# Half-by-half phases for the Fourier table, and a new hand-searched order, in a long-convolution and token-MLP kernel

## Chip, cores and metric

The kernel runs on one core of a Trainium2 chip. The metric is the device time of one execution in microseconds; 3 runs of the kernel before gave a median of 176.52 us (176.28 to 176.68).

## What is computed

Two blocks over a sequence of S = 2048 tokens with D = 448 channels in bfloat16, each behind a layer norm and with a residual. Cut to what matters:

```python
def A(q, k, v, shift_k, ssm_k, ssm_D):
    k_shift = sum over t < 4 of k_pad[:, t:t+S] * shift_k[:, 3-t]     # short causal convolution
    kv = k_shift * v
    y = irfft(rfft(pad(kv)) * rfft(pad(ssm_k)))[:S]                   # long causal convolution, length S, per channel
    return q * (y + kv * ssm_D)
def B(x, w1, b1, w2, b2):
    h = layernorm(x)                                                  # over D
    u = gelu(einsum("bsd,sf->bdf", h, w1) + b1)                       # mixes the tokens, F = 1792
    return transpose(einsum("bdf,fs->bds", u, w2) + b2)
h   = x + A(layernorm(x), ...)
out = h + B(layernorm(h), ...)
```

## The kernel before

The sequence index is split in two digits, 128 partitions times R = 16. The long convolution is a two-stage Fourier transform made of matmuls. Its stages have tags in the code:

- **tables** (emit_tables): the twiddle table E (128 x 32 x 128, fp16) is made on the chip. For each half h of it, VectorE multiplies a row of frequencies with a row of positions into integer phases (L827, 128 x 1024), adds a quarter turn for the second copy (L831, 128 x 1024) and masks both (L834, 128 x 2048); ScalarE then takes the sine (L837). Half 0 holds the positions 0 to 7, half 1 those from 8 to 15. Smaller tables (FW, MA, MB, MN) are made beside it on GpSimd, VectorE and ScalarE, and an identity matrix for transposes.
- **loads** (emit_loads): SP's queue brings in the kernel rows ssm_k (four loads, L877), k (four, L888), v (four, L891), the shift weights (three small ones, L880 and L883), the row D (L895) and the bias vectors (L898, L900).
- **kT**: TensorE transposes the kernel rows (L1028) with a few filler matmuls between (L1015), and copies (L731 on VectorE, L728 on ScalarE) bring them out of PSUM.
- **kv**: k is transposed (L956), convolved with the shift weights by matmuls with diagonal blocks (L982), and multiplied with v (L997, VectorE only).
- **k1, u1**: first Fourier stage of the kernel and of kv (L1049), with evacuations (L1059; L1057 adds the row D and is on VectorE only, for the group i = 0 of the kernel), and re-ordering DMAs from GpSimd and SP (L1065).
- **k2, u2**: second stage (L1084), scaled on evacuation (L729, L732) or copied (L728, L731).
- **i1**: products of the spectra on VectorE (L1150), first inverse stage on TensorE (L1167), evacuations, re-ordering DMAs (L1189; the last pair L1179). Beside it, bits of other work: statistics of the input's layer norm (**q**, L1225), transposes of E (**ct**, L1098), normalised rows (**xn**).
- **i2**: last inverse stage (L1285, L1293), gate and residual (L1302, L1304, L1312, L1322), second layer norm (L1340 to L1371).
- **mlp**: first layer with L1418 and L1428, GELU (L1408), second layer L1440 and the last addition L1443.

Nothing of the order is written out directly. Each operation is recorded with what it reads and writes, and a list scheduler (class _Sched, method schedule) simulates five engines with fixed estimates of each operation's time, and decides the order in which each engine's instructions are issued. Its priorities are the table WHEN: each step of a tag has one number, and of the operations that are ready the one with the lowest number goes first. The table WHERE says for each operation that ScalarE or VectorE could do which of them does it: "a" is ScalarE, "d" VectorE, "f" leaves it to the scheduler, which gives it to VectorE only when ScalarE has a backlog. Engines execute in the order so fixed, and wait on semaphores for what they need. An operation can have two kinds of predecessors: "after" stands for finished data, and "safter" only says that the other instruction must have been issued and run its estimated time in the plan; it adds no semaphore wait.

In the kernel before, the keys of the two halves of the phases are 79 and 73, and VectorE does them in turns: multiply of one half, multiply of the other, and so on.

Of the kernel before, what the change touches and what calls it, by code (L numbers as in the profile page):

```python
# [9 lines left out]

ENGS = ("pe", "act", "dve", "pool", "sp")
WHEN = {
    "dummy": (47,),
    "tables": (135, 108, 181, 171, 72, 79, 73, 180,),
    "loads": (107, 115, 122, 123, 200, 184, 83, 229, 88, 228, 168, 189, 218, 146, 156,),
    "kv": (207, 113, 131, 199, 132, 198, 48, 195, 226, 81, 103, 104, 75, 128, 136, 158, 185,),
    "kT": (61, 49, 202, 64, 222, 190, 152, 76,),
    "k1": (110, 116, 150, 183, 105, 134, 140, 163, 62, 87, 98, 133, 89, 194, 170, 169,),
    "k2": (82, 85, 70, 84, 129, 145, 91, 161, 193, 192, 175, 179, 100, 121, 182, 230,),
    "u1": (71, 80, 97, 126, 130, 155, 148, 173, 174, 176, 196, 219, 69, 90, 142, 209,),  # L20
    "xload": (263, 214, 5, 112,),
    "bias": (178, 216,),
    "q": (213, 241, 186, 251, 240, 231, 252, 272, 287,),
    "u2": (102, 114, 221, 268, 191, 177, 31, 45, 125, 144, 66, 162, 94, 101, 298, 224,),
    "ew": (120,),
    "i1": (77, 34, 43, 86, 53, 215, 59, 143, 65, 165, 19, 141, 18, 37, 67, 206, 54,),
    "ct0": (201, 38,),
    "ct": (223, 137, 20,),
    "xn": (68, 187, 307, 21, 36, 277,),
    "w1a": (299, 6, 303, 24,),  # L30
    "warm": (301, 294,),
    "i2": (74, 56, 281, 32, 188, 172, 40, 291, 106, 304, 264, 4, 3, 23, 7, 99, 160, 151, 204, 42, 225, 93, 293, 309,
        284, 197, 35, 159, 259, 14, 205, 118, 245, 220, 44, 302, 58, 288, 2, 12, 253, 271, 269, 262, 242, 166, 22,
        265, 16, 157, 292, 0, 39, 60, 232, 17, 236, 119, 283, 55, 267, 15, 92, 13, 111, 285, 249, 296, 308, 41, 300,
        26, 276, 95, 25, 282, 52, 279, 63, 30, 57, 310, 149, 117, 11, 273, 295, 305, 210, 46, 257, 203, 29, 127, 290,
        255, 124, 109, 306, 167, 212, 10, 8, 9, 211, 28,),
    "w1b": (280,),
    "w2": (208,),
    "mlp": (96, 27, 78, 51, 138, 1, 50, 147, 286, 153, 139, 164, 297, 33, 227, 289, 217, 154, 418, 419, 420, 421,
        422, 423, 424, 425, 426, 427, 428, 429, 430, 431, 432, 433, 434, 435, 436, 437, 438, 439,),  # L40
}
WHERE = {
    "kv": "ddaadfdd",
    "kT": "ddfdfddd",
    "k1": "faffaffadfaa",
    "k2": "addfffdaffdafffd",
    "u1": "fafdffafafddfffa",
    "bias": "f",
    "u2": "aafafaaaffffffaf",
    "i1": "aaffffffaffaafaa",  # L50
    "ct0": "f",
    "ct": "aaf",
    "xn": "dafa",
    "i2": "adfadafaafaf",
}


# [515 lines left out]
def _build(nc, A_q, A_k, A_v, A_shift_k, A_ssm_k, A_ssm_D, B_w1, B_b1, B_w2, B_b2, out):  # L573
# [54 lines left out]
    with ctx:  # L628
        sch = _Sched(nc, ctx, n_dma_sems=112, small_off=SMALL)
        op = sch.op  # L630
# [106 lines left out]
        def emit_tables():  # L737
            N8 = 8192.0
            SC = (2.0 * math.pi / N8) * (1.0 - 2e-6)
            HALF = 8 * 128  # L740
            NB = 3 * 128
            o_fr = small(512)
            o_s = small(64)
# [6 lines left out]
            bias = view(o_b, [4], f32)  # L750
# [17 lines left out]
            for x in range(2):  # L768
# [3 lines left out]
                   w=[(o_fr, 512, "fr")], n=128, est=160.0)  # L772
# [3 lines left out]
               w=[(o_JK, 4)], est=1500.0)  # L776
# [3 lines left out]
               n=128, est=190.0)  # L780
# [3 lines left out]
               n=128, est=190.0)  # L784
# [32 lines left out]
            for i in (10, 11):  # L817
# [2 lines left out]
                   r=[(o_p + 16, 4), (o_p + 4 * i, 4)], w=[(o_p + 16, 4)], n=1)  # L820
            op("dve", lambda e, W: e.tensor_copy(out=pcf[:, 0:6], in_=pc[:, 4:10]), r=[(o_p + 16, 24)],
               w=[(o_p + 48, 24)], n=6)
            for h in range(2):
                sch.t0 = T_TH if h else -40.0
                o_ph = (o_pi, o_TK)[h]
                ph = view(o_ph, [2, 8, 128], i32)
                op("dve", lambda e, W, h=h, ph=ph: e.tensor_tensor(  # L827
                    out=ph[:, 1], in0=frow.unsqueeze(1).broadcast_to([128, 8, 128]),
                    in1=srow[:, 8 * h:8 * h + 8].unsqueeze(2).broadcast_to([128, 8, 128]), op=ALU.mult),
                   r=[(o_fr, 512), (o_s, 64)], w=[(o_ph + 4096, 4096)], n=HALF, kind="1x")  # L830
                op("dve", lambda e, W, ph=ph: e.tensor_scalar(  # L831
                    out=ph[:, 0], in0=ph[:, 1], scalar1=2048, scalar2=None, op0=ALU.add),
                   r=[(o_ph + 4096, 4096)], w=[(o_ph, 4096)], n=HALF)
                op("dve", lambda e, W, ph=ph: e.tensor_scalar(  # L834
                    out=ph, in0=ph, scalar1=8191, scalar2=None, op0=ALU.bitwise_and),
                   r=[(o_ph, 8192)], w=[(o_ph, 8192)], n=2 * HALF)
                op("act", lambda e, W, h=h, ph=ph: e.activation(  # L837
                    out=E[:, 16 * h:16 * h + 16, :].rearrange("p a (b c f) -> p a b c f", b=4, c=2).rearrange("p a b c f -> p (a b) c f"),
                    in_=ph.rearrange("p c r (g f) -> p c (r g) f", f=16).rearrange("p c g f -> p g c f"),
                    func=ACT.Sin, bias=bias[:, 0:1], scale=-SC),  # L840
                   r=[(o_ph, 8192), (o_b, 4)], w=[(o_E + 4096 * h, 4096)], n=2 * HALF)
# [661 lines left out]
```

## Time and profile before

| what | us |
|---|---|
| median of 3 runs | 176.52 |
| the profiled execution | 176.59 |
| its span in the trace | 174.70 |
| last kernel rows' transposes begin on TensorE | 11.72 |
| first stage-one matmul of the kernel | 13.69 |
| last re-ordering transfer issued | 76.28 |
| last inverse stage goes on after it | 80.36 |
| second MLP layer begins | 129.39 |
| last instruction of the chain ends | about 172.3 |

Times are from one profiled execution, counted from the span's start. "Busy" of an engine leaves out waits and issue of DMAs. The chain of waits is followed back from the last instruction. TensorE's matmuls are pipelined and their ends are modelled. The granted TensorE clock was 1.00 throughout.

Some rows of the groups of instructions that matter below (mean duration of one, in ns): L827 1224, L831 690, L834 1222, L837 2020, L731 644, L1057 1089, L1059 913 on ScalarE and 1085 on VectorE, L1150 1082. Waiting times: GpSimd's re-ordering DMAs waited 12.5 us for ScalarE's evacuations of stage one and 10.2 us for those of the inverse stage; TensorE waited 3.3 us for the last re-ordering transfers.

### The profile page before, as it was taken

How to read it: one execution, taken by the hardware profiler on the slowest of the kernel's cores; microseconds unless marked ns; L12 is line 12 of the kernel's file. 1: busy time of each engine (PE TensorE's matmuls, PEld its weight loads, DVE VectorE, ACT ScalarE, POOL GpSimd, SP SyncE). 2: the span in 40 equal slices, each digit the busy share in tenths (PEclk: the TensorE clock that was granted, in tenths of full speed). 3: DMA queues.
4: the chain of work that ended last, by engine and by line, in shares of the span. 5: the costliest groups of instructions: out<-in, count | busy, mean ns of one | idle time of the engine just before them, and what ended most of it. 6: DMA issues, size and time to landing. Idle time of an engine off the chain costs nothing.

```text
span 174.7 us, 3576 instructions
## 1 busy us (share of the span) xinstructions
PE 161.2 (92%) x1419; PEld 92.7 (53%) x1419; DVE 103.6 (59%) x192; ACT 89.4 (51%) x128; POOL 62.4 (36%) x160
## 2 busy tenths in 40 slices
PE   6999999899989997756999999999999999999993
PEld 2776835352323332422344545555567777777783
DVE  7998899878979898988998561000003132132231
ACT  3786767888999999873792664521220000000000
POOL 8355708672902548774589660000000000000000
PEclk9999999999999999999999999999999999999999
DMA  5999846791948764559999999930000111101111
GB/s 174 408 310 370 285 154 263 278 356 60 271 142 312 243 208 119 163 127 367 381 391 403 421 420 422 420 152 0 0 0 4 53 53 53 53 0 56 53 53 53
DMA packets 15516, 35.15 MB, mean 201 GB/s; under 512 B 3804, under 2 KB 9580, under 8 KB 15500
## 3 DMA queue, kind: packets, MB, share of 16 engines
q1 hardware_dynamic: 12348, 28.15, 44.2%
q0 software_dynamic: 3008, 6.69, 11.9%
q8 instruction: 11, 0.18, 0.4%
q10 hardware_dynamic: 144, 0.08, 0.2%
q14 instruction: 5, 0.04, 0.1%
HBM read 22.05 MB, written 1.84 MB: 137 GB/s over the span
## 4 chain that ended last, share of the span: by engine, by line
PE 60%; ACT 9%; DMA 9%; DVE 7%; POOL 6%; issue 5%; SPq 1%; POOLq 0%; DVEq 0%
PE ps L1440 24%; PE ps L1428 12%; PE ps L1418 8%; ACT arena L728 5%; DMA arena<-arena 5%; DMA arena<-in_A_ssm_k_dram 4%; PE ps L1049 4%; PE ps L1084 3%; ACT arena L1059 3%; DVE arena L1312 3%; POOL arena L1189 3%; PE ps L1285 2%; DVE arena L1371 2%; PE ps L1167 2%; PE ps L982 2%
## 5 line engine op out<-in xcount | busy, mean ns | idle before, releaser
L1443 DVE SCALAR_TENSOR_TENSOR arena<-ps,arena 128x448 bf16<-128x448 f32 (+2 forms) x17 | 11.1, 656 | 55.6 <-PE ps L1440 55.6
L1440 PE MATMUL ps<-arena 128*128 128x448 bf16 (+2 forms) x238 | 42.7, 342 | 0.0
L1440 PEld LDWEIGHTS ps<-arena 128*128 128x128 bf16 x238 | 33.3, 145 | 9.5
L728 ACT CAST arena<-ps 128x896 bf16<-128x896 f32 (+1 forms) x31 | 25.0, 954 | 1.0 <-PE ps L925 0.5
L1418 PE MATMUL ps<-arena 128*128 128x448 bf16 x112 | 22.9, 353 | 0.1
L1059 ACT CAST arena<-ps 128x896 bf16<-128x896 f32 x23 | 19.5, 913 | 6.2 <-PE ps L1049 5.9
L1065 POOL DMA_DIRECT2D arena<-arena x32 | 17.5, 553 | 13.0 <-ACT arena L1059 12.5
L1428 PE MATMUL ps<-arena 128*128 128x448 bf16 x112 | 21.7, 353 | 0.0
L1150 DVE TENSOR_TENSOR arena<-arena 128x1792 bf16<-128x1792 bf16 x16 | 16.6, 1082 | 1.0 <-DMA arena<-arena 0.9
L1167 PE MATMUL ps<-arena 64*128 64x448 bf16 x128 | 14.5, 351 | 2.9 <-DVE arena L1150 2.2
L1408 ACT ACTIVATE arena<-ps,arena 128x448 bf16<-128x448 f32 x14 | 8.4, 635 | 17.2 <-PE ps L1428 17.0
L1084 PE MATMUL ps<-arena 128*64 128x448 bf16 x128 | 15.6, 359 | 1.6 <-DMA arena<-arena 0.9
L1418 PEld LDWEIGHTS ps<-arena 128*128 128x128 bf16 x112 | 10.5, 98 | 11.3 <-DVE arena L1371 1.8
L1428 PEld LDWEIGHTS ps<-arena 128*128 128x128 bf16 x112 | 10.9, 98 | 10.3 <-DVE arena L1304 0.3
L1049 PE MATMUL ps<-arena 128*32 128x448 bf16 x256 | 15.1, 355 | 0.6 <-DVE arena L997 0.3
L1189 POOL DMA_DIRECT2D arena<-arena x14 | 8.4, 600 | 10.6 <-ACT arena L728 10.2
L1084 PEld LDWEIGHTS ps<-arena 128*64 128x64 f16 x128 | 5.8, 108 | 10.7 <-ACT arena L728 2.7
L1167 PEld LDWEIGHTS ps<-arena 64*128 64x128 f16 x128 | 5.3, 94 | 11.6 <-ACT arena L728 5.9
L1285 PE MATMUL ps<-arena 128*128 128x448 bf16 x32 | 7.7, 353 | 3.7 <-DMA arena<-arena 3.3
L1302 ACT ACTIVATE arena<-ps,arena 128x448 f32<-128x448 f32 x9 | 6.5, 720 | 8.3 <-PE ps L1285 5.0
L1225 DVE BATCH_NORM_STATS2 arena<-arena 128x6 f32<-128x448 bf16 x16 | 9.4, 608 | 0.5 <-DMA arena<-in_A_q_dram 0.5
L1049 PEld LDWEIGHTS ps<-arena 128*32 128x32 f16 x256 | 5.0, 95 | 8.4 <-DVE arena L997 2.6
(98 smaller groups left out, 195.5 us busy)
## 6 DMA issues: line engine op xcount, KB each, us to landing
arena<-in_B_w_dram SPq DMA_DIRECT2D x8, 896.0 KB, 12.5
arena<-in_B_w_dram SPq DMA_DIRECT2D x2, 2048.0 KB, 17.3
arena<-arena SPq DMA_DIRECT2D x16, 224.0 KB, 3.4
arena<-arena POOLq DMA_DIRECT2D x32, 112.0 KB, 3.6
arena<-in_B_w_dram SPq DMA_DIRECT2D x2, 1536.0 KB, 18.9
arena<-arena POOLq DMA_DIRECT2D x14, 196.0 KB, 4.1
arena<-in_A_k_dram SPq DMA_DIRECT2D x4, 448.0 KB, 5.8
arena<-in_A_v_dram SPq DMA_DIRECT2D x4, 448.0 KB, 8.9
```

The costliest lines, as they stand in the source:

```text
L728: return e.copy(out=dst(), in_=src())
L1049: op("pe", lambda e, W, b=b, r=r, q=q, x=x, c0=c0: e.matmul(PS[32 * q:32 * q + 32, b.slots[x], 0:D], E[:, 2 * r + x, c0:c0 + 32], src[:, r ...
L1059: return e.copy(out=dst, in_=Ppair(b)) if W == "act" else e.tensor_copy(out=dst, in_=Ppair(b))
L1065: shuf[tag].append(op(q_, lambda e, W, g=g, i=i, a=a, nu=nu, jh=jh: e.dma_start(T[a + i:a + i + 4 * nu - 3:4].rearrange("p (j k) c d -> p ...
L1084: op("pe", lambda e, W, b=bs[h], h=h, j=j, c=c, par=par: e.matmul(PS[64 * par:64 * par + 64, b.slots[c], 0:D], FW[:, 64 * c:64 * c + 64], ...
L1150: op("dve", lambda e, W, m=m, i=i: e.tensor_tensor(out=MR(m.slots[0]).rearrange("p (x y) d -> p x y d", x=2), in0=TU[:, i].unsqueeze(2).br ...
L1167: k = op("pe", lambda e, W, b=bs[h], m=ms[h], par=par, t=t, tab=tab, xy=xy, P=P: e.matmul(Pb(b, par), tab[P, :], MR(m.slots[0])[P, xy, :], ...
L1189: shuf["z" + q_ + str(j)] = shuf["z" + q_] = op(q_, lambda e, W, j=j, p0=p0, a=a, b_=b_, j0=j0: e.dma_start(TZ[p0:p0 + 29:4, j0:j0 + (b_ - ...
L1285: k = op("pe", lambda e, W, b=b, r=r, h=h: e.matmul(Pb(b), ET[:, 2 * r + h, :], TZ[:, r, h, :], start=(h == 0), stop=(h == 1 and r >= NZ)) ...
L1418: op("pe", lambda e, W, r=r, fc=fc, b=bs[fc]: e.matmul(Pb(b), W1A[:, r, 128 * fc:128 * fc + 128], Q[:, r, :], start=(r == 0), stop=(r == R ...
L1428: op("pe", lambda e, W, r=r, fc=fc, b=b: e.matmul(Pb(b), W1B[:, r, 128 * (fc - n0):128 * (fc - n0) + 128], Q[:, r, :], start=(r == 0), sto ...
L1440: op("pe", lambda e, W, r=r, fc=fc, b=b, d0=d0, d1=d1: e.matmul(Pb(b)[:, d0:d1], W2[fc // 7][:, fc % 7, r:S:R], G[:, fc, d0:d1], start=(fc ...
```

## The change

Two things are changed. The first is in emit_tables: the multiply of the second half gets the mask instruction of the first half as a "safter" predecessor, so that the planner issues the second half's phases behind the whole of the first. The second is that all numbers of WHEN (but the last 22 of "mlp") and all letters of WHERE are replaced. No instruction is added or taken away by it apart from the choice of engine, and the tables' sizes stay.

```diff
 WHEN = {
-    "tables": (135, 108, 181, 171, 72, 79, 73, 180,),
-    "loads": (107, 115, 122, 123, 200, 184, 83, 229, 88, 228, 168, 189, 218, 146, 156,),
-    "kv": (207, 113, 131, 199, 132, 198, 48, 195, 226, 81, 103, 104, 75, 128, 136, 158, 185,),
-    "kT": (61, 49, 202, 64, 222, 190, 152, 76,),
-    "k1": (110, 116, 150, 183, 105, 134, 140, 163, 62, 87, 98, 133, 89, 194, 170, 169,),
+    "tables": (95, 198, 242, 202, 238, 62, 160, 153,),
+    "loads": (69, 82, 98, 171, 232, 201, 203, 244, 106, 246, 195, 197, 223, 250, 93,),
+    "kv": (243, 144, 149, 75, 262, 141, 163, 233, 80, 85, 90, 79, 148, 158, 92, 190, 237,),
+    "kT": (175, 64, 104, 49, 214, 140, 210, 68,),
+    "k1": (139, 145, 155, 228, 103, 151, 157, 234, 61, 87, 136, 199, 81, 152, 170, 204,),
...
-    "u2": (102, 114, 221, 268, 191, 177, 31, 45, 125, 144, 66, 162, 94, 101, 298, 224,),
-    "i1": (77, 34, 43, 86, 53, 215, 59, 143, 65, 165, 19, 141, 18, 37, 67, 206, 54,),
-    "ct": (223, 137, 20,),
+    "u2": (71, 78, 249, 188, 156, 164, 15, 21, 154, 108, 14, 147, 30, 66, 293, 256,),
+    "i1": (6, 48, 115, 116, 187, 212, 167, 122, 129, 174, 150, 83, 169, 63, 130, 58, 59,),
+    "ct": (208, 302, 247,),
...
 WHERE = {
-    "kv": "ddaadfdd",
-    "kT": "ddfdfddd",
-    "k1": "faffaffadfaa",
-    "k2": "addfffdaffdafffd",
-    "u1": "fafdffafafddfffa",
-    "bias": "f",
-    "u2": "aafafaaaffffffaf",
-    "i1": "aaffffffaffaafaa",
-    "ct0": "f",
-    "ct": "aaf",
-    "xn": "dafa",
-    "i2": "adfadafaafaf",
+    "kv": "ddffafdd",
+    "kT": "fdfadddf",
+    "k1": "afddfafadafa",
+    "k2": "addaafdfdfdafdad",
+    "u1": "faaaaaffafddfaaf",
+    "bias": "a",
+    "u2": "aaaaaaaaaafdafaa",
+    "i1": "faaffffaaaaffafa",
+    "ct0": "d",
+    "ct": "ffd",
+    "xn": "afff",
+    "i2": "afdafdafadff",
 }
...
+            ph_last = []
             for h in range(2):
                 sch.t0 = T_TH if h else -40.0
...
-                   r=[(o_fr, 512), (o_s, 64)], w=[(o_ph + 4096, 4096)], n=HALF, kind="1x")
+                   r=[(o_fr, 512), (o_s, 64)], w=[(o_ph + 4096, 4096)], n=HALF, kind="1x", safter=tuple(ph_last))
...
-                op("dve", lambda e, W, ph=ph: e.tensor_scalar(
+                ph_last.append(op("dve", lambda e, W, ph=ph: e.tensor_scalar(
                     out=ph, in0=ph, scalar1=8191, scalar2=None, op0=ALU.bitwise_and),
-                   r=[(o_ph, 8192)], w=[(o_ph, 8192)], n=2 * HALF)
+                   r=[(o_ph, 8192)], w=[(o_ph, 8192)], n=2 * HALF))
```

The loads in the order of the table are: four kernel-row loads; the three shift loads (one number); k and v blocks in the order k3, k0, v0, k1, v1, k2, v2, v3; the row D; the two bias vectors (one number). The entries of "tables" for the two halves of the phases are the sixth and the seventh.

## Prediction

> **What bounds the kernel now.** I read the busy shares first, then the chain of waits, then a table of busy time by stage, then VectorE's instructions at the start.
>
> ```profile
> PE 161.2 (92%) x1419; PEld 92.7 (53%) x1419; DVE 103.6 (59%) x192; ACT 89.4 (51%) x128; POOL 62.4 (36%) x160
> ```
>
> TensorE is busy for 92% of the span. The chain says from where on nothing else matters (columns: start, length, what):
>
> ```profile
> 2.58 7.83 DMA arena<-in_A_ssm_k_dram
> ...
> 10.46 0.96 PE ps L1028 x12
> ...
> 13.76 1.63 PE ps L1049 x32
> ...
> 76.28 3.73 DMA arena<-arena
> ...
> 80.36 2.44 PE ps L1285 x12
> ...
> 111.23 18.16 PE ps L1428 x96
> 129.39 42.09 PE ps L1440 x231
> ```
>
> From about 80.4 us on TensorE does the last convolution stage and the MLP almost without a gap. That part has a fixed length, since neither its matmuls nor its loads change. The end therefore moves with one moment: the landing of the last re-ordered block (issued at 76.28, landed at 80.01). The question is what the new order does to the first 80 us. The stages before it (columns: stretch, its length, then busy us of TensorE, weight loads, VectorE, ScalarE, GpSimd; clock; DMA):
>
> ```profile
> 7.20:13.70 6.50, 6.32 (x78) 4.93 (x78) 6.32 (x15) 5.51 (x6) 4.12 (x7) 1.00 1.04 340
> 13.70:24.50 10.80, 10.49 (x237) 7.22 (x240) 9.65 (x16) 7.02 (x9) 5.51 (x11) 1.00 0.92 307
> 24.50:35.00 10.50, 9.78 (x202) 4.50 (x194) 9.44 (x13) 8.65 (x11) 6.47 (x13) 1.00 0.59 227
> 54.00:65.00 11.00, 10.42 (x100) 4.33 (x98) 10.52 (x15) 10.67 (x14) 4.96 (x9) 1.00 0.80 261
> 65.00:76.00 11.00, 7.60 (x78) 3.37 (x72) 10.38 (x24) 10.48 (x14) 9.07 (x15) 1.00 0.46 138
> ```
>
> Up to 35 us TensorE and VectorE are full and ScalarE has room (3.8 us idle in 13.7 to 24.5). After 54 us VectorE and ScalarE are both full. At the very start VectorE is full too:
>
> ```profile
> 2.22 1.23 DVE L827 TENSOR_TENSOR arena<-arena 128x1024 int32<-128x1024 int32 x1
> 3.36 0.16 DVE L812 TENSOR_TENSOR arena<-arena 128x8 int32<-128x8 int32 x1
> 3.44 1.22 DVE L827 TENSOR_TENSOR arena<-arena 128x1024 int32<-128x1024 int32 x1
> ...
> 7.20 1.22 DVE L834 TENSOR_SCALAR arena<-arena 128x2048 int32<-128x2048 int32 x1
> 8.33 0.69 DVE L731 COPY arena<-ps 128x1024 bf16<-128x1024 bf16 x1
> ...
> 11.04 2.66 DVE L731 COPY arena<-ps 128x1024 bf16<-128x1024 bf16 x5
> ```
>
> The six phase instructions fill 2.22 to 8.42 us. The copies of the transposed kernel rows come behind them, the last ending at 13.70. The first kernel matmul (L1049) starts at 13.69.
>
> **The change part by part.**
>
> *Phases half by half.* The same six instructions stay: 2 x (1.22 + 0.69 + 1.22) = 6.3 us. In turns, the halves are complete at 7.21 and 8.42. One after the other, the first is complete 3.1 us after it starts, at about 5.3, the second at about 8.5. What is new is that each instruction needs the one directly before it. The row: independent L812 starts at 3.36, 0.09 before L827 ends at 3.45. The dependent cast L802 starts at 1.92, 0.03 after L800 ends at 1.89. That is 0.12 per link, four links, 0.5 us. The Trainium skill, "VectorE: DVE Perf Modes", section "The DRAIN you can't avoid", says that chaining without semaphores saves nothing: eight copies took the same time with a semaphore after each as with one at the end. By it the cost is 0. I take the row, since the overlap stands in it: at most 0.5, less where a small table instruction sits between. Its cover is the wait for kernel rows, which VectorE has in any case; if that cover is gone, it is 0.5 on the path. Behind these self-waits stand only the small table instructions and the kernel-row copies, whose rows land later anyway. The early half itself gains nothing: the kernel stage also needs all kernel rows (landed 11.72) transposed and copied.
>
> *Order of the loads.* Read from the new keys, SP's queue becomes: two kernel-row loads, the two bias vectors, a third, one k block, the fourth kernel-row load, k, v, k, k, v, the three shift loads, v, v, and the D row last. No bytes are added and every issue still counts (about 0.45 each, in all about 9.5 us). Before, two k blocks (2 x 448 KB) go ahead of the kernel rows, now one. At the 403 GB/s of 4.4 to 7.2 us, one block is 1.1 us, so the last kernel rows land at about 10.5 instead of 11.72. Against this stand the bias vectors, now ahead of two of these loads. The row is where small loads were under way: 213 GB/s in 9.0 to 10.5 us, at a DMA share of 1.12, so (403 - 213)/403 x 1.5 = 0.7 us lost. The skill's "DMA: Bandwidth & Descriptors" section "Specifications", gives 512 B as the least transfer for line rate, below which the engine reads, modifies and writes. Taking that as half rate (an estimate), the 7.5 KB (3.5 + 4.0) of the bias vectors cost 0.04 us and the landing stays at 10.5; by the row it is 11.2. I take the 10.5: the lost 0.7 is shared with the other small loads and was paid before the last kernel rows landed in this trace too, so it is inside the 11.72 (bounds 0 and +0.7). From landing to the first kernel matmul it was 1.97 us (11.72 to 13.69), so the stage can start at about 12.4.
>
> *GpSimd's constants.* The frequency iotas (key 95) now go before the identity's (198), so the phases can start at about 1.6 instead of 2.22, and the identity is ready at about 3.2 instead of 1.9; the first rows land at 4.4. Cost 0, +0.3 if that cover is gone.
>
> *Engines.* Of the eight kernel-row copies six were fixed to VectorE and none to ScalarE; now four and one, three free. ScalarE was idle from 2.5 to 5.4. Three copies moved cost ScalarE 3 x 0.95 and spare VectorE 3 x 0.65 = 2 us, which keeps VectorE from being later than the load. The k transposes (40 in 4.57 to 6.97) move the other way: TensorE does them later.
>
> *What the earlier start is worth.* If TensorE's later work is conserved and dense, 0. If all of the 1.3 us (13.7 - 12.4) carries, 1.3. Between 4.4 and 13.7 TensorE ran about 2.7 us of filler matmuls (L1015), which real work can replace, and ScalarE's 3.8 us idle in the next stage can take kernel evacuations. I take the middle, -0.6.
>
> *The middle orders.* All convolution and evacuation keys change. The work of the evacuation engines is conserved; fixed choices go from 38 to 47 for ScalarE and 23 to 26 for VectorE, so freedom falls, but sums hardly change. Between 13.7 and 54 us VectorE is idle for 5.3 us and ScalarE for 6.9. I take cost 0, and as bounds a tenth of these 12.2 us either way, -1.2 and +1.2.
>
> *The end of the first convolution.* Before, ScalarE copies a transposed table at 74.14 for 1.03 us although the last matmul group, begun at 73.42, ends at 74.35; the evacuation that the last transfer needs waits until 75.05, some 0.65 us. That group waited for its product (L1150) at 71.97, behind statistics. Now the last pair's products have keys 58 and 59 (before 206 and 54), ahead of nearly everything on VectorE, and one of three table copies is fixed to VectorE (0.66 for such a copy at 62.87). Worth 0 to -0.65 unless products then displace other groups; I take -0.3. The keys of the last stages and of the weight loads change too, but the loads stay chained in their order, and TensorE is full: 0, bounds -0.2 and +0.6 (its idle time in 80.4 to 93.6 is 0.5).
>
> *Sum.* The profiled execution took 176.59 us: span 174.70 and 1.89 around it; the median 176.52 is 0.07 lower. 176.59 - 0.6 - 0.3 = 175.7; on the median's scale 175.6.
>
> **The rivals.**
>
> *The D row comes too late (slower).* It is now last in SP's queue. The v loads took 8.9 us to land (median of four), the last issued at about 9.7, so D lands at about 18.6. Four kernel evacuations (L1057) can only run on VectorE and add D; VectorE runs in order, so behind such a wait stand all its copies and the convolution products (L997), and two PSUM banks stay held. Before, the first came at 24.71. If its new place is reached at 15.4, VectorE stands for 3.2 us in a stretch where it is 89% busy; half of that, as ScalarE takes the other half, is 1.6, and 175.7 + 1.6 = 177.3. It decides from a wait of about 1.8 us on, where half of it eats the 0.9. For it: the place in the queue. Against it: the keys of the first (139) stand behind other kernel groups, and VectorE has other work.
>
> *The new late order is worse (slower).* The last group to be re-ordered is one that sends two large GpSimd transfers (4.1 us to landing, one more issue of 0.6) instead of the small kind (3.2), and one more statistic and product come before it: 0.9 + 0.6 + 0.6 = 2.1, without the gain of the end: 176.59 - 0.6 + 2.1 = 178.1; with half of that, 177.0. I take 177.6. For it: VectorE and ScalarE are full there (95%), so any misplacement shows. Against it: the last pair's inputs still have the last keys (291, 309).
>
> *No effect.* TensorE is dense from 13.7 to 24.5 (10.49 of 10.80), the delayed k transposes eat the early start, and the end is as before: 176.5. That the phases are made half by half and nobody is waiting for the first half belongs here.
>
> **How the numbers follow.** A change of 0.2%, 0.35 us, is about the least that measurement of this kernel can tell from none. Faster (175.6, own range 174.5 to 176.1): 0.47. No effect (176.2 to 176.8): 0.10. D row late (177.3): 0.20; late order worse (177.6): 0.23; slower together 0.43, from 176.9 to 179. Since the slower cases hold nearly half, the range goes from 174.5 to 178.2; I leave out about 0.05 below and 0.13 above.
>
> **What would show it.** Right: phases of one half complete at about 5.3; last kernel-row landing at about 10.5; first L1049 at about 12.4; the last re-ordering transfer landed near 79; no VectorE wait for the D row over 1 us. TensorE from there as before, 94 us to the end. Wrong: L1049 at 13.5 or later, a long VectorE wait for D, ScalarE as idle as before in the stage after the start, or a last transfer after 80.4.

## The result and the profile after

The kernel after the change took 185.13 us (median of 4 runs, 185.03 to 186.18) against 176.6 for the kernel before (176.28 to 176.82): ratio 1.0522, 95% interval [1.0478, 1.0566]. The prediction was 175.6, faster, with a range up to 178.2. Later, 44 more runs of the same kernel, in two sets beside other kernels, had medians of 178.55 and 179.53 and never reached 184. So two things need explaining: about 1.7 us that the new order costs where the TensorE clock stays full (the table at the end of the experiments), and the rest, which comes and goes. Medians below are over all runs of a kernel; the intervals of ratios leave out runs more than 1.5% above their kernel's fastest.

The profiled execution of the first set took 186.18 us (span 183.9). The row of the granted TensorE clock, 40 slices of 4.6 us, shows what was new. In the profile of before it is 9 throughout:

```profile
PEclk9996999999999999697599999999999999999999
```

The chain of waits (start, length, what; all lines from L827 on are one higher than before):

```profile
7.98 11.38 DMA arena<-in_A_shift_k_dram
...
38.92 0.96 PE ps L1085 x8
...
81.22 6.69 DMA arena<-arena
87.96 4.67 PE ps L1286 x14
...
120.77 18.16 PE ps L1429 x96
138.93 42.08 PE ps L1441 x231
```

It starts at the shift weights instead of the kernel rows. The second Fourier stage (L1085) starts 3.8 us later than before, the last re-ordering transfer lasts 6.69 us instead of 3.73, and the matmuls behind it 4.67. From L1429 to the end the two kernels are alike. By stretches (columns as in the prediction's table; the clock is the third value from the end):

```profile
14.00:16.50 2.50, 2.50 (x32) 1.05 (x32) 1.34 (x3) 0.91 (x1) 0.00 (x0) 0.50 1.06 378
74.70:78.10 3.40, 3.40 (x25) 2.14 (x21) 2.29 (x6) 2.01 (x3) 3.07 (x6) 0.51 0.68 202
82.00:88.00 6.00, 0.42 (x4) 0.05 (x2) 2.65 (x9) 0.74 (x2) 3.20 (x7) 0.74 0.97 297
88.00:91.60 3.60, 3.60 (x10) 1.44 (x11) 1.53 (x5) 1.16 (x2) 0.35 (x1) 0.50 1.06 383
```

TensorE ran at half clock in three of these stretches, and in the third row it stood nearly idle. In the second row it is busy all the time and yet slow: the evacuations that GpSimd's last transfers wait for come late. GpSimd at the end of the inverse stage (start, length, line; in brackets the idle time and who ended it), and below it SP:

```profile
80.40 0.66 POOL L1180 DMA_DIRECT2D arena<-arena  x1 [2.50 <-ACT arena L728]
81.22 0.61 POOL L1180 DMA_DIRECT2D arena<-arena  x1
```

```profile
78.62 2.19 SPq L1180 DMA_DIRECT2D arena<-arena  x2
81.09 2.56 SPq L1392 DMA_DIRECT2D arena<-in_B_w_dram  x4
```

The pair of last groups has four transfers, two from GpSimd and two from SP. The first weight load (L1392, 896 KB) is released by one of them, SP's earlier one (issued at 78.62); it does not wait for GpSimd's two. Here it went out at 81.09, 0.13 us ahead of GpSimd's second transfer, which then took 6.69 us to land. In the kernel before, GpSimd's second transfer had 0.54 us of lead (76.28 against 76.82).

### The profile page after: what moved, and what is told of

It is laid out like the page before. It is cut to its first block, busy times and chain, and to the rows that moved or that the text cites. A ratio compares the mean times of both kernels' runs of the same rounds, so it can differ in the third digit from the quotient of the medians.

```text
span 183.9 us, 3570 instructions
## 1 busy us (share of the span) xinstructions
PE 165.8 (90%) x1419; PEld 95.3 (52%) x1419; DVE 103.4 (56%) x191; ACT 90.2 (49%) x129; POOL 65.6 (36%) x160
## 3 DMA queue, kind: packets, MB, share of 16 engines
q0 software_dynamic: 3008, 6.69, 11.8%
## 4 chain that ended last, share of the span: by engine, by line
PE 61%; DMA 13%; ACT 11%; POOL 5%; SPq 4%; issue 3%; DVE 2%; DVEq 0%; POOLq 0%
PE ps L1441 23%; PE ps L1419 12%; PE ps L1429 12%; DMA arena<-arena 6%; DMA arena<-in_A_shift_k_dram 6%; ACT arena L728 5%; PE ps L1286 4%; PE ps L1050 3%; ACT arena L729 3%; ACT arena L1060 3%; PE ps L1168 2%; PE ps L1085 2%; PE ps L983 2%; POOL arena L1190 1%; POOL arena L862 1%
## 5 line engine op out<-in xcount | busy, mean ns | idle before, releaser
L1066 POOL DMA_DIRECT2D arena<-arena x32 | 17.7, 558 | 16.5 <-ACT arena L1060 15.8
L1419 PE MATMUL ps<-arena 128*128 128x448 bf16 x112 | 22.9, 353 | 0.0
L1429 PE MATMUL ps<-arena 128*128 128x448 bf16 x112 | 21.7, 352 | 0.0
L1085 PE MATMUL ps<-arena 128*64 128x448 bf16 x128 | 15.3, 359 | 2.7 <-DMA arena<-arena 1.5
L1050 PE MATMUL ps<-arena 128*32 128x448 bf16 x256 | 16.2, 377 | 1.2 <-DVE arena L998 0.6
L1151 DVE TENSOR_TENSOR arena<-arena 128x1792 bf16<-128x1792 bf16 x16 | 16.7, 1084 | 0.8 <-ACT arena L728 0.8
L1419 PEld LDWEIGHTS ps<-arena 128*128 128x128 bf16 x112 | 10.8, 98 | 10.7 <-DVE arena L1372 1.2
L1429 PEld LDWEIGHTS ps<-arena 128*128 128x128 bf16 x112 | 11.0, 98 | 10.2
L1286 PE MATMUL ps<-arena 128*128 128x448 bf16 x32 | 9.6, 424 | 6.4 <-DMA arena<-arena 5.6
L1085 PEld LDWEIGHTS ps<-arena 128*64 128x64 f16 x128 | 5.7, 108 | 11.7 <-ACT arena L728 3.2
L731 DVE COPY arena<-ps 128x1024 bf16<-128x1024 bf16 (+2 forms) x14 | 8.8, 649 | 3.9 <-PE ps L957 1.2
L1050 PEld LDWEIGHTS ps<-arena 128*32 128x32 f16 x256 | 5.5, 100 | 9.8 <-DVE arena L998 3.0
```

Source lines behind the costliest of these rows:

```text
L1050: op("pe", lambda e, W, b=b, r=r, q=q, x=x, c0=c0: e.matmul(PS[32 * q:32 * q + 32, b.slots[x], 0:D], E[:, 2 * r + x, c0:c0 + 32], src[:, r ...
L1066: shuf[tag].append(op(q_, lambda e, W, g=g, i=i, a=a, nu=nu, jh=jh: e.dma_start(T[a + i:a + i + 4 * nu - 3:4].rearrange("p (j k) c d -> p ...
L1085: op("pe", lambda e, W, b=bs[h], h=h, j=j, c=c, par=par: e.matmul(PS[64 * par:64 * par + 64, b.slots[c], 0:D], FW[:, 64 * c:64 * c + 64], ...
L1151: op("dve", lambda e, W, m=m, i=i: e.tensor_tensor(out=MR(m.slots[0]).rearrange("p (x y) d -> p x y d", x=2), in0=TU[:, i].unsqueeze(2).br ...
L1286: k = op("pe", lambda e, W, b=b, r=r, h=h: e.matmul(Pb(b), ET[:, 2 * r + h, :], TZ[:, r, h, :], start=(h == 0), stop=(h == 1 and r >= NZ)) ...
L1419: op("pe", lambda e, W, r=r, fc=fc, b=bs[fc]: e.matmul(Pb(b), W1A[:, r, 128 * fc:128 * fc + 128], Q[:, r, :], start=(r == 0), stop=(r == R ...
```

## The experiments

In the kernels below the planner's order is edited after it is made (the list `order`), so all the rest of the order stays. "z00" and "z10" are GpSimd's two transfers of the last pair, "z01" and "z11" SP's; the weights wait for "z11". The first theory was: the order of that pair on GpSimd, together with the weights' release by one transfer, costs the 8.5 us. The later experiments showed that this is only the last link.

**The phases alone, in the kernel before.**

```diff
+ids = self.mark["ph"]
+pos = sorted(order.index(i) for i in ids)
+for p, i in zip(pos, ids[3:] + ids[:3]):
+    order[p] = i
```

> The kernel before, in its own order; only VectorE's six phase instructions are put half by half (half 1 first, as its half came first before). Theory (the phases themselves are harmless; the loss comes from the new order around them): within 0.4 us of 176.6, since VectorE waits for kernel rows anyway; the four links cost up to 0.5 us by the row of before. Rival (half by half is what costs): the first kernel matmul comes 2 us or more later and the time is 179 or more.

Measured 176.62 us (21 runs, 174.54 to 179.75) beside 176.26 for the kernel before: 0.9999 [0.9973, 1.0025]. Alone, half by half changes nothing that could be told (0.3% either way).

**GpSimd's two transfers exchanged**, in the kernel after and in the kernel before, each measured twice:

```diff
+a, b = order.index(self.mark["z00"]), order.index(self.mark["z10"])
+order[a], order[b] = order[b], order[a]
```

> The changed kernel with two GpSimd transfers exchanged and nothing else: of the last pair's two, the one that is ready first is issued first. Theory (the ready transfer stood in GpSimd's queue behind one that waited, and so came 0.13 us after the first weight load instead of before it): both are issued before the weights, the last lands near 84 instead of 87.9, TensorE's wait is short enough that its clock stays full, and the time falls by 4 to 6 us, to 179 to 181. Rival (the order of the two doesn't matter, the memory is busy with weights in any case): the other transfer lands late instead, 184.5 to 185.5.

> The same kernel as a_zorder (the changed one, with the last pair's two GpSimd transfers exchanged), in five rounds, since its two times lay far apart (176.74 and 181.19). Theory (the exchange takes away nearly all of the loss; what is left is the later conv start, and now and then a half clock of TensorE): median 176.5 to 178, at most 2 us above the kernel before. Rival (176.74 was luck, the rest of the new order costs 4 us): 180 to 182.

> The kernel before with the one fault put in: the last pair's two GpSimd transfers are exchanged, so that the ready one stands behind the one that waits; nothing else differs. Theory: the ready one is issued at about 76.9, at the time of the first weight load (76.82) or behind it, lands 5 to 7 us later instead of 3.7, TensorE waits long enough for a half clock, and the time rises by 3 to 8 us, to 180 to 184. Rival (the loss needs the rest of the new order): within 1 us of 176.3.

> The kernel before with the last pair's two GpSimd transfers exchanged, again. Theory (in this order the later GpSimd transfer always comes after the release of the weight loads, since GpSimd first waits for ScalarE): lost in every run, 182 to 186 us, no run at a mean clock of 0.99 or above. Rival (that exchange too only tips a balance, as it does in the kernel after): a part of the runs at clock 0.99 to 1.00 and at 176 to 179 us.

In the kernel after: 176.74 and 181.19 in the first set; then 14 runs, median 178.46 (176.57 to 183.08), 1.007 [1.0034, 1.0106]. I read this as nearly the whole loss undone. That was wrong, since I compared with the 185.13 of another set; the unchanged kernel had 178.55 and 179.53 in later sets. What the exchange does in the kernel after is within what the sets differ by.

In the kernel before, the exchange loses in every run: 184.1 (4 runs, 183.14 to 185.22; 1.0455 [1.0403, 1.0506]) and again 183.6 (6 runs, 182.3 to 184.08; 1.042 [1.0384, 1.0455]), mean clock 0.972 to 0.981 in all ten, as the first theory said. Of the first of these, GpSimd and the chain:

```profile
75.68 0.66 POOL L1182 DMA_DIRECT2D arena<-arena  x1 [1.64 <-ACT arena L731]
76.50 0.76 POOL L1182 DMA_DIRECT2D arena<-arena  x1
```

```profile
76.50 8.45 DMA arena<-arena
```

The weight loads began at 76.25. A transfer issued 0.25 us behind the first of them took 8.45 us; in the second set 0.15 us behind, 6.83. So the last link is real: in the kernel before, losing the lead costs 7 to 8 us.

**The weights wait for all four transfers.**

```diff
+if o.tag == "w1a":
+    for x in ("z00", "z01", "z10", "z11"):
+        self.dep(W, self.ops[self.mark[x]].ev)
```

> The changed kernel, but the first weight load waits until all four transfers of the last pair have landed (before: only one of them). Theory (the last transfer is slow because weights are queued ahead of it): it lands 3.2 us after its issue, near 84.5, and the last inverse stage goes on there; the weights start 3.4 us later, at about 84.5, which may cost the MLP's start a part: 180.0 to 182.5. Rival (the transfer is slow by itself): it still takes about 6 us, weights come later still, 187 or more.

Measured 179.36 (179.11 and 179.61; 1.0178 [1.0121, 1.0236]). The transfer landed in 2.70 us, but the weights went out at 82.07 and TensorE waited 0.8 us for them. Two runs, and the control only in other sets (178.55 and 179.53 us): the wait makes the transfer quick, and whether it is worth or costs anything in all is not shown. In the kernel before, waiting for one more transfer ("z01" in the same edit):

> The kernel before with one more wait: the first weight load also waits until SP's own later transfer of the last pair has landed, about 2 us after the one it waits for now. Theory (weights compete with the last re-ordering transfer in the kernel before too): the transfer lands in about 2.8 us instead of 3.73, TensorE goes on about 0.9 us earlier, the weights come 2 us later and just in time; 0.994 to 1.000 of the kernel before. Rival (the MLP's first matmul then waits for its weights): 1.003 or more.

Median 175.74 (14 runs, 175.19 to 176.8) beside 176.7: 0.999 [0.9957, 1.0023]. It holds the weights to 78.64, and the last transfer lands in 2.67 us instead of 3.73, as expected; the time stays the same. No version here is shown to beat the kernel before.

**Fillers against the falling clock.** Twenty-six more matmuls ahead of those that wait for the last transfer, into the PSUM bank that these then start afresh; nothing of them reaches a result.

```diff
+for _ in range(n_):
+    self.issue(W, self.eng[W].matmul(self.PS[:, o.bufs[0].slots[0], 0:448], lhs, rhs, start=True, stop=True))
```

> The changed kernel with 26 filler matmuls (0.19 us each at full clock, 4.9 us in all) on TensorE in the gap before the matmul that waits for the last transfer. Theory (the half clock after the gap is a cost of its own): the clock is full after the gap, the 14 matmuls behind it take about 2.8 us instead of 4.66, and the time falls by 1.5 to 2 us, to 183.2 to 183.7. Rival (the evacuations set the pace there, not the clock): the matmuls are quicker, but the first MLP matmul comes less than 0.5 us earlier; 184.7 to 185.2.

> The changed kernel with 26 filler matmuls, now ahead of TensorE's wait for the last transfer (in a_warmz they stood behind it, and cost their own length). Theory (the half clock after the long gap is a cost of its own, about 2 us of the 8.5): the clock is full when the transfer has landed, the 14 matmuls behind it take 2.8 us instead of 4.66, and the time falls from 185.1 to 182.8 to 183.6. Rival (evacuations set the pace there): 184.6 or more.

In the first (183.86; 185.17 and 182.55) they came behind the wait instead of into it (from 82.17 on, the transfer having landed at 82.13), so it tells only what they cost. In the second: 180.7 (4 runs, 179.68 to 184.35; 1.025 [1.0162, 1.0338]). The clock was 1.00 in its profile, but so it was in half of the control's runs without fillers, and the fillers stood on the chain themselves:

```profile
79.06 5.06 PE ps L544 x26
```

**The order of the loads, with the exchange in place.** First before's load order (SP's queue as before, but with the D row last; the conversions of the bias vectors moved back, since these now land later; the rest as after), then after's with the three shift loads moved up to directly behind the fourth kernel-row load; `ids` are the load operations in the wanted order:

```diff
+for p, i in zip(pos, ids):
+    order[p] = i
```

> a_zorder with the loads of the start in the order of the kernel before (the D row alone stays last, and the two bias conversions that need the later bias vectors are moved behind the first kernel matmuls). Theory (the shift weights, landing 2 to 4 us later in the changed kernel, hold the short convolution and everything behind it): the convolution's first matmul (L982 of before) at about 19.3 instead of 20 to 22, and 0.7 to 2 us less than a_zorder_5. Rival (TensorE is full there and the order of loads doesn't matter): within 0.5 us of a_zorder_5.

> a_zorder with the three shift-weight loads moved forward in SP's queue, right behind the last kernel rows; nothing else. Theory (what is left after the exchange comes from the start: the conversion of the late shift weights stands in GpSimd's queue ahead of the first re-ordering transfers, and the short convolution waits for them): the weights land by 14, the first re-ordering transfers leave 2 us earlier, and the time falls by about 1 us below a_zorder_5, to the level of the kernel before (0.995 to 1.003 of it). Rival (small loads, moved forward, slow the large ones behind them, or the start is hidden): 1.006 or more.

Before's load order gave 181.28 (178.66 to 184.72; 1.0197 [1.0143, 1.025]), a miss: the after order puts kernel-row transposes first on TensorE, and with k loaded first they wait (first kernel matmul at 17.20). Loads and TensorE's order belong together. Early shift weights gave 177.95 (16 runs, 176.98 to 181.41; 1.0108 [1.007, 1.0147]), no gain either. Why, is on GpSimd:

```profile
16.61 1.35 POOL L1073 DMA_DIRECT2D arena<-arena  x2 [3.92 <-ACT arena L1067]
17.95 0.22 POOL L942 CAST arena<-arena 128x16 f32<-128x16 bf16 x1
```

The cast of the shift weights (L942) now found its data landed (issued from 4.1 to 5.4, 7.2 to 8.1 us to land). It stood behind the first re-ordering transfers, which waited 3.92 us for ScalarE.

**Without the "safter" line**, so that the planner plans anew:

> The changed kernel without the one structural line: the second half's multiply has no order behind the first half's mask, so the phases go in turns again, under the new keys; the planner then orders everything else somewhat differently too. Theory (the phases' order is worth under 0.5 us by itself, but the keys were chosen with it): between 178 and 187, decided by whether the last pair's transfers again stand in the wrong order on GpSimd. Rival (half by half is the cost): 177 or less.

198.48 us (197.68 and 199.27), 1.127 [1.1197, 1.134]. The keys were found with that line; without it the same numbers are a different and far worse order. It says nothing about the phases themselves.

**The phases back in turns**, in the kernel after, the rest of the order untouched:

```diff
+m0, a0, k0, m1, a1, k1 = self.mark["ph"]
+for x, y in ((m1, m0), (a1, a0), (k1, k0)):
+    order.remove(x)
+    order.insert(order.index(y) + 1, x)
```

> The changed kernel with only VectorE's phase instructions put back in turns, in its own order otherwise. Theory (the phases' order is not what costs): within 0.7 us of 185.1. Rival (half by half costs at the start): 183.5 or less.

179.72 (4 runs, 178.49 to 180.98; 1.0214 [1.0129, 1.03]), where my theory had 185. Either the phases cost 5 us, or the kernel after was not 185 in that set. So the kernel after itself was run again beside it:

> The kernel after the change itself, unchanged, on the chip and beside the runs of the three kernels that follow. Theory (two upsets that each come or stay away with the landing times of a run: the half clock at 13 to 17 us because the last kernel rows land late, worth about 2.2 us, and the late last pair of re-ordering transfers, worth 5 to 7 us): spread, runs anywhere from 177 to 186 us and not all at 185; a profiled run with a full clock at the start has its first product before 51.5 us. Rival (the phases half by half are themselves what costs): all runs within 0.7 us of 185, and the kernel with the phases in turns 5 us below it in the same runs.

> The kernel after the change with only the phases of the large table put back in turns, again, beside the unchanged kernel. Theory: the same spread and median as the unchanged kernel, within 1.5 us of its median. Rival: near 179.7 us again, 5 us below the unchanged kernel.

The control: 178.55 (22 runs, 176.81 to 183.61; 1.0049 [1.0021, 1.0078] to 177.13 for before). In turns, in the same set: 180.43 (22 runs, 177.84 to 189.75; 1.0125 [1.0092, 1.0159]). So half by half is about 0.8% *better* in the new order (the medians lie 1.9 us apart, where 1.5 at most was expected; between the runs at full clock it is 0.8 us). Where that comes from is read from the traces. VectorE in the kernel after (start, length):

```profile
3.64 1.21 DVE L835 TENSOR_SCALAR arena<-arena 128x2048 int32<-128x2048 int32 x1
4.78 1.21 DVE L828 TENSOR_TENSOR arena<-arena 128x1024 int32<-128x1024 int32 x1
...
5.99 0.68 DVE L731 COPY arena<-ps 128x1024 bf16<-128x1024 bf16 x1
6.66 0.69 DVE L832 TENSOR_SCALAR arena<-arena 128x1024 int32<-128x1024 int32 x1
```

The first kernel-row copy runs between the halves, at 5.99. In turns (the second run of it) it comes at 8.45, and TensorE waits for it:

```profile
9.18 0.47 PE L1035 MATMUL ps<-arena 128*128 128x128 bf16 x4 [2.06 <-DVE arena L736]
```

**Fillers at the start**, without and with the exchange (the same call as above, 11 matmuls in four places), in the control's set:

> The kernel after the change with 11 more filler matmuls ahead of the kernel rows' transposes and of the first kernel matmuls, where TensorE waits for loads anyway (in none of the results). Theory: the granted clock stays 1.0 through 12 to 17 us, the first product of 53.62 us comes before 51.5, and the median lies 1 to 4 us under the unchanged kernel's; the last pair can still be late, so single runs above 180 stay possible. Rival (the clock at the start costs nothing at the end): no fall, within 0.7 us of the unchanged kernel.

> The same fillers together with the exchange of the last pair's two GpSimd transfers. Theory: both upsets are gone, 176 to 177.5 us in nearly every run, spread under 2 us, the kernel before within 0.5%. Rival (something else of the new order costs too): 178.5 us or more, as the exchange alone gave in its median.

182.44 (6 runs, 179.43 to 187.08; 1.017 [1.0101, 1.024]) and 180.55 (179.09 to 182.33; 1.0158 [1.0098, 1.0218]): both slower than the control, though neither profile has half clock at the start (the first has no record of the clock, but its long matmuls keep starting 0.18 to 0.19 us apart). The first kernel matmul came at 14.97 and 15.14, where the control had 14.43, since the last two fillers ran after the rows were there. That is 0.54 us of the 0.96 by which the profiled 179.43 is above the control's 178.47; the rest, and why the medians are 2 to 4 us above the control's, is not settled. The sign that the expectations named, a first product (L1151) before 51.5 us at full clock, failed too: 52.50 in the control and 53.37 with fillers. My theory that the two upsets are the whole loss fell here.

**The control once more**, beside the second measurement of the exchanged kernel before:

> The unchanged kernel after the change once more, in another set of runs. From the 22 runs of the control: 176.8 to 178.6 us at a mean clock of 1.00, and about 2 us more for every 0.01 of mean clock lost (0.99 about 179.9, 0.98 about 182, 0.97 about 183.6). Theory (the loss is counted in stretches of half clock, how many come is a matter of the landing times of a run): the same line again, each run within 1.2 us of it, whatever the median turns out to be. Rival (the 185 us of the first runs and the 178.5 of the control are two chips' speeds, the clock only goes along): runs at clock 1.00 well above 179 us, or runs at 0.97 below 181.

179.53 (22 runs, 176.65 to 182.14; 1.0102 [1.0073, 1.0132] to 176.26). All 48 runs of the kernel after, by mean clock of the run rounded to hundredths, beside 140 runs of the kernel before from the experiments' sets:

| mean clock | after: runs, median us | before: runs, median us |
|---|---|---|
| 1.00 | 23, 178.15 | 111, 176.42 |
| 0.99 | 17, 179.83 | 25, 177.23 |
| 0.98 | 3, 181.83 | 4, 179.86 |
| 0.97 | 3, 185.03 | none |
| 0.96 | 2, 185.66 | none |

A stretch of 3.4 us at half clock in 178 us is 0.0096 of mean clock, so the rows count such stretches. A straight line through the 48 runs gives 2.08 us for each 0.01. Matmuls at half speed alone can make 1.78 of it (0.01 of 178 us, an estimate); the rest goes with the gaps that come with the half clock. The expectation asked for every run within 1.2 us of the line; of the second control's 22 runs 17 are. Two at full clock are well above it (179.76, and 181.57 at 0.999), as the rival said: the clock is the larger part of the spread and not the whole. Slower chips it is not: the kernel before had 176.26 to 177.13 beside these kernels in every set, and 176.6 beside the first four runs. The first four runs had three or four stretches each; why all of those, and only one of 44 later, stays open.

## Why the prediction was wrong

Three executions side by side, all in us; the middle one is the control's, at clock 1.00 (178.47 us):

| moment | before | after, clock 1.00 | after, clock 0.963 |
|---|---|---|---|
| last kernel rows' transposes begin | 11.72 | 12.64 | 12.07 |
| first kernel matmul (L1050, 32) | 13.69 | 14.43 | 14.30 |
| first convolution (L983) | 19.32 | 21.15 | 21.93 |
| second stage of the kernel (L1085) | 35.10 | 37.80 | 38.92 |
| GpSimd's last transfer | 76.28 | 78.49 | 81.22 |
| inverse stage goes on (L1286) | 80.36 | 82.02 | 87.96 |
| second layer, 96 matmuls (L1429) | 111.23 | 113.06 | 120.77 |
| span | 174.7 | 176.2 | 183.9 |

*Phases half by half* and *GpSimd's constants*: right. The phases began at 1.57; the first half took 3.28 us, to 4.85, for 3.14 of work (two links in 0.14), with small table instructions in the links, and the second was complete at 8.65. What I missed is that a kernel-row copy fits between the halves.

*Order of the loads, and the earlier start (-0.6)*: failed. The last kernel rows' transposes began at 12.07 and 12.64, not 10.5, and the first kernel matmul at 14.30 and 14.43, not 12.4. One k block fewer went ahead, and the landing did not come sooner. The prediction put the 213 GB/s of 9.0 to 10.5 us down to the small loads under way there, and took it as paid already. In the kernel after, the bias vectors had landed by 6.1 us, and the dip stands all the same, and longer (DMA share and GB/s are the last two values):

```profile
4.40:7.20 2.80, 2.80 (x25) 2.27 (x24) 2.80 (x6) 2.01 (x1) 1.99 (x10) 1.00 1.03 376
7.90:10.40 2.50, 1.89 (x21) 1.31 (x19) 2.19 (x5) 2.45 (x3) 0.00 (x0) 1.00 1.08 203
10.40:12.00 1.60, 1.30 (x21) 1.01 (x21) 0.76 (x3) 1.60 (x2) 1.42 (x4) 1.00 0.95 222
```

So these small loads do not make this dip; what does, stays open. In the profiles of the experiments that kept this load order and this start the transposes began anywhere from 11.02 to 12.51, so from run to run the moment varies by more than the gain that I had reckoned.

*The middle orders (0, bounds 1.2 either way)*: the term that was mis-sized first. At full clock the delay grows from 0.74 us at the first kernel matmul to 2.70 at the second stage, 1.96 us. I costed the engines' sums and not what the new order queues behind what. GpSimd, before and then after at clock 1.00:

```profile
12.62 1.28 POOL L861 TENSOR_TENSOR arena<-arena 128x128 f16<-128x128 f32 x3 [2.09 <-ACT arena L852]
...
15.61 0.20 POOL L934 CAST arena<-arena 128x16 f32<-128x16 bf16 x1 [1.19 <-DMA arena<-in_A_shift_k_dram]
16.40 1.36 POOL L1065 DMA_DIRECT2D arena<-arena  x2 [0.59 <-ACT arena L1059]
```

```profile
17.13 1.35 POOL L1066 DMA_DIRECT2D arena<-arena  x2 [3.61 <-ACT arena L1060]
18.66 0.20 POOL L935 CAST arena<-arena 128x16 f32<-128x16 bf16 x1 [0.18 <-DMA arena<-in_A_shift_k_dram]
18.83 2.26 POOL L862 TENSOR_TENSOR arena<-arena 128x128 f16<-128x128 f32 x3
21.04 1.13 POOL L1066 DMA_DIRECT2D arena<-arena  x2
```

Three small table instructions (L862) used to run before the re-ordering transfers. Now they and the cast stand behind the first two, which wait 3.61 us for ScalarE, and the cast also stands behind loads that land 10.84 us after issue; and the next two transfers stand behind all of that, at 21.04. The chain of the control runs through exactly this: shift weights, L862, L1066, then TensorE at 25.86. The run with early shift weights shows that removing one of the two waits leaves the other. No run put L862 back ahead of the transfers: that this queue makes the 1.96 us is read from the chain and not tested.

*The end of the first convolution (-0.3)*: right when the clock holds. One table copy is now on VectorE (75.21 in the control), and the last evacuation begins at 76.47, 0.07 us behind its matmuls instead of 0.70. From the second stage to GpSimd's last transfer it is 40.69 us at clock 1.00 against 41.18 before, and the total delay falls from 2.70 to 1.66. That is why the full-clock loss is 1.7 us (178.15 against 176.42) and not 2.7. *The late order* rival (177.6) thus came near the full-clock time by luck, for another reason than it gave; *the D row* was not it: it landed at 20.45, and its first user (L1058) came at 26.65.

*"The granted clock was 1.00" and "that part has a fixed length"*: the assumption that cost most. From the middle to the right column the delay at L1085 grows by 1.12 (half clock from 13.2 to 16.6), at GpSimd's last transfer to 2.73 (half clock in 74.7 to 78.1), at L1286 to 5.94 (a transfer of 6.69 instead of about 3.4), and at L1429 to 7.71 (14 matmuls in 4.67 instead of 2.82). These 7.7 us and the 1.8 of the order make the 9.54 between the outer columns. The prediction had no term for the clock at all.

The links, as far as shown: a slow TensorE delays ScalarE's evacuation, GpSimd loses its lead on the weight loads (1.02 us in the control, -0.13 here), the late transfer leaves TensorE idle, and the clock falls again. The exchanged kernel before shows the part from the lost lead on; the part ahead of it is read from this one trace. How idleness and clock go together shows in two executions of the same kernel, the control at clock 1.00 and then the second control:

```profile
80.00:82.00 2.00, 0.55 (x3) 0.10 (x1) 2.00 (x8) 0.01 (x1) 1.31 (x4) 1.00 0.78 191
82.00:85.40 3.40, 2.82 (x14) 1.29 (x14) 2.97 (x12) 2.38 (x5) 2.29 (x4) 1.00 1.01 380
```

```profile
80.00:82.00 2.00, 0.22 (x2) 0.14 (x3) 1.74 (x6) 0.00 (x0) 1.28 (x4) 1.00 0.82 224
82.00:85.40 3.40, 3.40 (x12) 1.43 (x11) 2.02 (x6) 1.96 (x4) 1.62 (x3) 0.60 1.04 397
```

With a gap of 1.47 us the clock stayed, with one of 2.2 us it fell. The length of the gap alone does not decide, though. In the profile of the kernel after it fell behind a gap of 1.81 us (72.49 to 74.29), and in the exchanged kernel before, second set, it stayed behind one of 2.08 (74.27 to 76.36). Two stretches of the first, then two of the second:

```profile
71.24:74.65 3.41, 1.60 (x16) 0.58 (x14) 2.79 (x8) 3.41 (x6) 2.65 (x5) 1.00 0.49 136
74.65:78.06 3.41, 3.41 (x27) 2.14 (x21) 2.30 (x6) 2.02 (x3) 3.12 (x6) 0.50 0.68 203
```

```profile
71.34:74.75 3.41, 2.93 (x36) 1.80 (x34) 3.41 (x9) 2.90 (x5) 2.83 (x5) 1.00 0.62 180
74.76:78.17 3.41, 1.81 (x10) 0.99 (x11) 2.63 (x11) 2.53 (x4) 2.12 (x5) 1.00 0.41 100
```

These stretches lie on a grid that the traces show. In each of the 19 profiles with a record of the clock, its changes lie whole multiples of 3.413 us apart, and where that grid begins differs from execution to execution. Divided by it, the profiles have 899 windows at full clock. TensorE was busy for less than 45% of 12 of them, and half clock followed on all 12; between 45 and 50% on 3 of 8; above 50% on 2 of 879. A gap that lies within one window thus counts, and one cut by a grid line (the 2.08 us) counts less, so the place of the grid makes much of the difference between two runs of one kernel. This is counted in the profiles and was not tested by a run. The two exceptions (71 and 76% busy) are both the start's transposes, 9.6 to 13.2 us, with the fall at 13.2 and 13.0; they stay open.

The Trainium skill, "TensorE: Matmul & The Clock Gate", section "Part 1: The HAM clock gate", has the rate halve after a free-running window of some 3.4 us in which TensorE was idle. The window's length and that it runs free agree; but here windows in which TensorE was busy for 35 to 49% were followed by half clock too, and the measurement decides.

## What to carry to other kernels

When a plan is replaced as a whole, equal sums mean little: list for each in-order queue which instruction now stands behind which wait, GpSimd's small instructions and DMA issues first. Look for the places where a release is a matter of tenths of a microsecond (here a bulk load released by one of four transfers), because a small delay anywhere above can tip them. And measure the unchanged kernel beside every experiment: several of my early readings compared with a number from another set, and the control took them back.

## What the runs showed of the hardware

- A 98 KB transfer from GpSimd, issued 0.13 to 0.25 us behind the first of four 896 KB loads from SP, took 6.69, 6.83 and 8.45 us to land. Issued about 0.5 us ahead of it (five profiles) it took 3.73 to 4.91, 0.7 to 1.1 us ahead 3.28 to 3.67, and 1.4 us or more ahead 2.67 to 2.90.
- The three shift-weight loads (0.5 to 3 KB) in SP's queue behind 448 KB loads took 10.8 to 12.2 us to land; moved up in the queue 7.2 to 8.1.
- The TensorE clock fell to 0.50 for 3.4 us, or twice that, after idle gaps as short as 1.8 us, on a grid of 3.413 us, where TensorE had been busy for less than about half of one window. Each such stretch went with about 2 us of a run of the kernel after. The same program had between none and four of them.
